# A start through two DMA queues, and 1 MB loads in four pieces

## The chip, the cores and the metric

The kernel runs on one core of a Trainium2 chip. The core has a matmul engine (TensorE; PE in the profile, and PEld for its weight loads), a vector engine (VectorE, DVE), a scalar engine for activations (ScalarE, ACT), GpSimd (POOL) and a sync engine (SP) that does little but issue transfers. ACT can issue transfers too, in line with its other instructions (ACTq in the profile). Each engine takes its instructions strictly in the order written, and waits for others by semaphores. Transfers move through 16 DMA engines between the main memory, in which inputs, outputs and scratch lie, and the on-chip memory (SBUF); matmul results land in eight banks of PSUM, from where DVE or ACT copies them out. The metric is the device time of one execution in microseconds.

## The reference: what is computed

The input x is 2048 tokens by 1024 features in bf16. Four blocks follow one another, each a residual step on the normalised x: A, B, A, B, with the weights of A and B used twice. `_layernorm` has no learned scale.

```python
x = A_x
x = x + _A_ref(_layernorm(x, axis=-1), A_wqkv, A_w_phi, A_wo)
x = x + _B_ref(_layernorm(x, axis=-1), B_wqkv, B_wo)
x = x + _A_ref(_layernorm(x, axis=-1), A_wqkv, A_w_phi, A_wo)
x = x + _B_ref(_layernorm(x, axis=-1), B_wqkv, B_wo)
return x
```

A is linear attention with 32 heads of 32 features: queries and keys go through a small matrix phi per head, then softmax over the features of that and of its negative gives 64 features; the state is the sum over tokens of these features times values, and each query reads the state and divides by its own sum. B is ordinary softmax attention over all 2048 tokens with 32 heads of 32, without a mask. Each block ends in a 1024 x 1024 projection.

## The kernel before

x is held transposed on the chip (`xT`: features on the 128 partitions in 8 groups `po`, tokens along the row), and the tokens are worked in 4 chunks of 512 (`C512`). One pass over A then B is called a layer here; there are two. All other on-chip data lie in one big tile, `arena`, in which a small allocator places buffers; a buffer's class has a quota and a queue.

The start, which the change touches most:

- `load_x` brings x in by transposing transfers. Chunk 0 is 8 transfers of 128 x 512, chunk 1 another 8, and chunks 2 and 3 together 8 of 128 x 1024, all on SP (L516).
- `fold_phi` for the keys loads the key weights in two halves of 1 MB through ACT's queue (L604), transposes them on PE in 8 groups g (L613), casts each group out of PSUM (L621 on ACT, L618 on DVE), multiplies with phi (L640) and casts the results into two slabs of folded weights (L647 on ACT, L650 on DVE). The slabs are also stored to scratch (L654) for layer 2. Queries are folded the same way later, with transposing transfers (L627) in the place of PE's transposes.
- `slab` loads a slab of weights, 128 x 8 x 512 (1 MB) or 128 x 8 x 128 (256 KB), as one transfer on SP (L585). Its third result is a list of four dependencies, one for each pair of the 8 groups `po`; before, all four are the same transfer.
- `layernorm` of a chunk squares x on ACT (L539) in `n` parts, sums x and its squares over the features by matmuls with a constant matrix (L481 with onesD), forms the inverse deviation (L560 to L567) and applies it on DVE in four pairs of steps (L573, L577). With n=4 the first part starts when its quarter of x is there; with n=2 there are two parts.
- `a_keys` of a chunk: for two halves of the features and four groups of 128 tokens, keys and values by matmuls (L481), exponentials on ACT (L689), sums, reciprocals and scaled values on DVE (L693 to L702), and the state by small matmuls (L722).

After A's queries and projection come B's keys, queries and values, and the attention loop: scores (L1105) into PSUM, exponentials on ACT (L1114, some on DVE by a polynomial, L1048 to L1062), and products with the values and sums (L1146). Between these the planner fits matmuls of other work (L485). While layer 1's attention runs, layer 2's A already takes the keys of chunks 0 to 2; their normed chunks are stored to scratch (L1372) and loaded again when needed (L1263, 1 MB each).

The order of all instructions is the work of a planner at build time. Each piece of work is an `op` with an engine, an assumed duration, a priority (a due time) and its dependencies and buffers. `Sched.run` steps through an assumed time, and whenever an engine is free it takes the ready op with the lowest priority whose buffers can be placed. For transfers it assumes a fixed latency of 2 us and one that grows with the size (`kb`), partly in one line for all queues. The instructions are then issued in the order found, so any change to an op's pieces, sizes or priorities can move work anywhere behind it. What the planner assumes of times enters the order only. Semaphore waits follow from the data, and from eight semaphores which transfers use in turn: a transfer waits until the last one with its semaphore has landed.

Of the kernel before, what the change touches and what calls it, by code (L numbers as in the profile page):

```python
# [20 lines left out]
C512 = 512  # L21
# [315 lines left out]
def kernel(  # L337
# [11 lines left out]
    nc = tc.nc  # L349
# [44 lines left out]
    for j in range(4):  # L394
# [4 lines left out]
        out=rep[:].rearrange("p (x j) -> p x j", j=4),  # L399
        in_=J_bf[:].rearrange("p (j d) -> p d j", d=32)[:, 0:8, :],  # L400
    )
    nc.vector.tensor_copy(out=fold[:], in_=ident[:, 0:32])
    for a in range(1, 4):
        nc.vector.tensor_tensor(
            out=fold[:], in0=fold[:], in1=ident[:, 32 * a:32 * a + 32], op=ALU.add
# [4 lines left out]
        out=selb[:].rearrange("p (j d) -> p j d", d=32),  # L410
        in_=pick[:].unsqueeze(2).to_broadcast([P, 4, 32]),
    )
    for a in range(4):
        for j in range(4):
            c = (j + a) % 4
            nc.vector.tensor_copy(
                out=selr[32 * a:32 * a + 32, 32 * c:32 * c + 32], in_=selb[32 * a:32 * a + 32, 32 * j:32 * j + 32])
# [18 lines left out]
    xd_v = xd[:].rearrange("p (c o n) -> p c o n", c=3, o=PO)  # L436
# [31 lines left out]
    ANY = [(x,) for x in (7, 6, 5, 4, 3, 2, 1, 0)]  # L468
# [6 lines left out]
    def dma(prio, fn, deps=(), bufs=(), q="SP", kb=256, issue=0.55):  # L475
        return op(q, issue, fn, deps, bufs, prio, lat=2.0 + kb / 200.0)
# [34 lines left out]
    def load_x():  # L511
        for lo, hi, prio, us, kb in ((0, 1, -24.0, 1.3, 128), (1, 2, -9.0, 1.3, 400), (2, NC, -8.0, 2.0, 800)):
            last = []
            for po in range(PO):
                last.append(dma(
                    prio, lambda lo=lo, hi=hi, po=po: nc.sync.dma_start_transpose(  # L516
                        out=xT[:, po, lo * C512:hi * C512], in_=A_x[0, lo * C512:hi * C512, po * P:(po + 1) * P]),
                    issue=us, kb=kb))
            for c in range(lo, hi):
                xdone[c] = last  # L520

# [60 lines left out]

    def slab(cls, prio, src, n, deps=(), q="SP"):
        b, v = sb(cls, PO, n)
        o = dma(prio, lambda: (nc.sync if q == "SP" else nc.scalar).dma_start(out=v(), in_=src),  # L585
                deps, [b], q=q, kb=2 * n)
        return b, v, [o] * 4


    def slab_turned(cls, prio, src, n):  # L590
# [9 lines left out]
    def fold_phi(col, wd_v, prio, use_pe):  # L600
        w_t = []
        if use_pe:
            nb, nv = sb("wnat", PO, D)
            ld = [dma(-20.0, lambda h=h: nc.scalar.dma_start(  # L604
                out=nv()[:, :, C512 * h:C512 * h + C512], in_=A_w[:, :, col + C512 * h:col + C512 * h + C512]),
                (), [nb], q="AQ", kb=1024) for h in range(2)]
            for g in range(G):
                tb, tv = ps("wt", ANY)

                def tr(g=g, tv=tv):  # L610
                    o = tv().bitcast(BF16)
                    for po in range(PO):
                        nc.tensor.transpose(  # L613
                            out=o[:, po * P:(po + 1) * P], in_=nv()[:, po, g * P:(g + 1) * P], identity=ident[:])
                t1 = op("PE", 8 * 0.11, tr, [ld[g // 4]], [tb, nb], prio, mode="n")
                wb, wv_ = sb("wT", D)
                if g % 2:
                    t2 = op("DVE", dve_us(1024), lambda tv=tv, wv_=wv_: nc.vector.tensor_copy(  # L618
                        out=wv_(), in_=tv().bitcast(BF16)), [t1], [tb, wb], prio)
                else:  # L620
                    t2 = op("ACT", act_us(1024), lambda tv=tv, wv_=wv_: nc.scalar.copy(  # L621
                        out=wv_(), in_=tv().bitcast(BF16)), [t1], [tb, wb], prio)
                w_t.append((wb, wv_, t2))
        else:
            for g in range(G):
                wb, wv_ = sb("wT", D)
                t2 = dma(prio, lambda g=g, wv_=wv_: nc.sync.dma_start_transpose(  # L627
                    out=wv_(), in_=A_wqkv[:, col + g * P:col + (g + 1) * P]), (), [wb], issue=1.6)
                w_t.append((wb, wv_, t2))
        slabs = []  # L630
        for fc in range(2):
            s_b, s_v = sb("slab", PO, C512)
            parts = []
            for m in range(PO):
                pb, pv = ps("wt", ANY)

                def fn(m=m, pv=pv, fc=fc):
                    for k in range(4):
                        g = 4 * fc + k
                        nc.tensor.matmul(  # L640
                            pv()[:, k * P:(k + 1) * P], lhsT=w_t[g][1]()[:, m * P:(m + 1) * P],
                            rhs=phi()[:, g, :], start=True, stop=True)
                a = op("PE", 4 * 0.1, fn, [w_t[4 * fc + k][2] for k in range(4)] + phi_ld,
                       [pb, phi_b] + [w_t[4 * fc + k][0] for k in range(4)], prio + 0.01, mode="n")
                eng = ("ACT", "DVE")[m % 2]
                if eng == "ACT":
                    e = op("ACT", act_us(512), lambda m=m, pv=pv, s_v=s_v: nc.scalar.copy(  # L647
                        out=s_v()[:, m, :], in_=pv()), [a], [pb, s_b], prio + 0.01)
                else:
                    e = op("DVE", dve_us(512), lambda m=m, pv=pv, s_v=s_v: nc.vector.tensor_copy(  # L650
                        out=s_v()[:, m, :], in_=pv()), [a], [pb, s_b], prio + 0.01)
                parts.append(e)
            fs = slice(fc * C512, (fc + 1) * C512)
            st = dma(prio + 0.02, lambda s_v=s_v, fs=fs: nc.sync.dma_start(out=wd_v[:, :, fs], in_=s_v()),  # L654
                     parts, [s_b], kb=1024)
            slabs.append((s_b, s_v, [[parts[2 * i], parts[2 * i + 1]] for i in range(4)], st))
        return slabs
# [554 lines left out]
    xnA, xnB = {}, {}  # L1212
# [20 lines left out]
    for layer in range(2):  # L1233
# [14 lines left out]
            wv_s = [wv_slab(base + fc * 0.5, fc) for fc in range(2)]  # L1248
            chunks = range(NC - 1, NC)
        for c in chunks:  # L1250
            xnA[c] = layernorm(c, base + 10 * c - 9 if base + c else -16.0, ANY, n=4 if layer else 2)
            a_keys(c, base + 10 * c, wk_s, wv_s, kv, ANY)
        state = a_state(kv, base + 32)

        if layer == 0:
            wq_s = fold_phi(0, wdq_v, base + 15, False)
            store["q"] = [s[3] for s in wq_s]
        else:
            wq_s = [slab("slab", second - 15 + fc, wdq_v[:, :, fc * C512:(fc + 1) * C512], C512, [store["q"][fc]])
                    for fc in range(2)]  # L1260
            for c in range(NC - 1):
                x_b, x_v = sb("xn", PO, C512)
                xnA[c] = (x_b, x_v, [dma(second - 20 + 20 * c, lambda c=c, x_v=x_v: nc.sync.dma_start(  # L1263
                    out=x_v(), in_=xd_v[:, c, :, :]), [xnA[c]], [x_b], kb=1024)] * 4)
        wo_s = [slab_turned("slab", second - 6 + fc, A_o[:, :, fc * C512:(fc + 1) * C512], C512) for fc in range(2)]
        bv_s = [slab("slab", second - 4 + 134 * fc, B_w[:, :, 2 * D + fc * C512:2 * D + (fc + 1) * C512], C512)
                for fc in range(2)]
# [149 lines left out]
```

## Time and profile before

| what | value |
|---|---|
| median of 3 runs | 2376.43 us (2372.92 to 2377.3) |
| profiled execution | 2378.41 us, span 2376.6 us |
| granted matmul clock, mean | 0.994 |
| busy share of the span | PE 94%, ACT 87%, DVE 69%, POOL 1% |
| transfers | 118.58 MB, mean 50 GB/s |

A row of the instructions in time has the start in us, the duration, the engine, the line, what is written from what, how many follow each other (x), and in brackets how long the engine sat idle before and what ended that. A row of the waits has the waiter, what it waited for, the total in us, how often, and the longest. A row of busy time by stretch has, for each engine, busy us and the number of instructions, then the granted clock, the share of time in which the DMA engines were busy, and GB/s. "issue" is time in which an engine waited for nothing that the profile shows.

### The profile page before, as it was taken

What the parts mean: (1) busy time and instruction counts of PE and PEld (TensorE: products, weight loads), DVE (VectorE), ACT (ScalarE), POOL (GpSimd) and SP (SyncE); (2) the same over time, 40 slices, a digit from 0 to 9 for tenths busy, and PEclk for the clock granted to TensorE, in tenths of its full rate; (3) what the DMA queues carried; (4) which work ended last, traced back from release to release, by engine and by line L of the source; (5) the groups of instructions that cost most, each with busy time, mean ns of one, the idle gap of its engine ahead of it and who ended that gap; (6) DMA issues with size and microseconds to landing.
All of it is one profiled execution on the core that took longest, in us unless ns stands there. A gap on an engine that the chain in (4) does not pass through costs nothing. (4 is left out here: it accounts for less than half of the span.)

```text
span 2376.6 us, 65432 instructions
## 1 busy us (share of the span) xinstructions
PE 2243.0 (94%) x28906; PEld 846.6 (36%) x28976; DVE 1647.7 (69%) x2111; ACT 2073.2 (87%) x1852; POOL 25.4 (1%) x70
## 2 busy tenths in 40 slices
PE   7999999999999998999998999999999999989998
PEld 4443343333333333333333444433333333333333
DVE  7987752345678676775754786477778888978763
ACT  5436559999999999999996555899999999999998
POOL 0000000000000000000000000000000000000000
PEclk9999999999999999999999999999999999999999
DMA  9210101112221222213313101011111100111111
GB/s 217 64 34 1 32 21 33 28 38 64 63 80 54 56 60 69 82 56 91 126 56 98 37 3 34 22 36 27 35 26 38 34 20 24 56 35 36 38 36 38
DMA packets 218085, 118.58 MB, mean 50 GB/s; under 512 B 139208, under 2 KB 208840, under 8 KB 217032
## 3 DMA queue, kind: packets, MB, share of 16 engines
q1 hardware_dynamic: 215720, 112.29, 17.6%
q8 instruction: 226, 3.70, 0.6%
q10 hardware_dynamic: 2080, 2.10, 0.3%
q14 instruction: 59, 0.48, 0.1%
HBM read 78.71 MB, written 14.14 MB: 39 GB/s over the span
## 5 line engine op out<-in xcount | busy, mean ns | idle before, releaser
L1114 ACT ACTIVATE arena<-psum 128x1536 bf16<-128x1536 f32 x1297 | 1752.8, 1699 | 18.5 <-PE psum L1105 15.9
L1146 PE MATMUL psum<-arena 128*32 128x512 bf16 x4096 | 629.2, 385 | 11.8 <-DVE arena L1162 10.3
L1146 PE MATMUL psum<-arena,ones_bf 128*32 128x512 bf16 x4096 | 628.9, 385 | 0.0
L1105 PE MATMUL psum<-arena 32*128 32x512 bf16 x3890 | 512.8, 383 | 80.2 <-ACT arena L1114 70.3
L485 PE MATMUL psum<-arena 128*32 128x512 bf16 (+1 forms) x8768 | 580.7, 376 | 8.3 <-DVE arena L991 2.5
L481 PE MATMUL psum<-arena 128*128 128x512 bf16 (+1 forms) x1969 | 445.2, 374 | 10.1 <-issue 3.7
L1105 PEld LDWEIGHTS <-arena 32*128 32x128 bf16 x3890 | 173.4, 91 | 584.3 <-issue 573.9
L1059 DVE SCALAR_TENSOR_TENSOR arena<-arena 128x1024 f32<-128x1024 f32 x309 | 376.8, 1220 | 4.2 <-DMA arena<-arena 0.2
L485 PEld LDWEIGHTS <-arena 128*32 128x32 bf16 x8768 | 195.4, 96 | 236.0 <-issue 117.1
L481 PEld LDWEIGHTS <-arena 128*128 128x128 bf16 x2032 | 190.3, 98 | 243.3 <-issue 44.7
L1146 PEld LDWEIGHTS <-arena 128*32 128x32 bf16 x4096 | 167.0, 95 | 253.8 <-issue 198.5
L1048 DVE TENSOR_SCALAR arena<-psum 128x512 int32<-128x512 f32 x206 | 141.8, 688 | 102.0 <-PE psum L1041 91.2
L921 DVE CAST arena<-psum 128x512 bf16<-128x512 f32 x120 | 82.6, 688 | 176.5 <-PE psum L485 167.4
L1146 PEld LDWEIGHTS <-ones_bf 128*32 128x32 bf16 x4096 | 163.5, 95 | 31.8 <-issue 13.1
L1062 DVE SCALAR_TENSOR_TENSOR arena<-arena 128x1024 bf16<-128x1024 f32 x103 | 125.9, 1222 | 3.4 <-PE psum L1146 0.2
L689 ACT ACTIVATE arena<-psum 128x512 bf16<-128x512 f32 x80 | 43.0, 597 | 87.5 <-PE psum L481 66.6
L1381 PE MATMUL psum<-xT,zero 128*32 128x512 bf16 x1428 | 116.9, 383 | 0.0
L1162 DVE COPY arena<-psum 128x512 f32<-128x512 f32 x126 | 86.3, 685 | 34.3 <-PE psum L1146 33.7
L1203 DVE TENSOR_TENSOR arena<-arena 64x512 bf16<-64x512 f32 x124 | 84.7, 683 | 29.7 <-DMA arena<-rd 24.0
L693 DVE TENSOR_REDUCE arena<-arena 128x32 f32<-128x1024 bf16 x64 | 77.6, 1213 | 28.6 <-ACT arena L689 28.4
L815 ACT ACTIVATE arena<-psum 128x512 bf16<-128x512 f32 x128 | 69.4, 598 | 31.3 <-PE psum L481 29.1
L573 DVE TENSOR_TENSOR arena<-xT,arena 128x1024 f32<-128x1024 bf16 x64 | 77.8, 1219 | 23.8 <-ACT arena L562 23.8
(102 smaller groups left out, 1369.2 us busy)
## 6 DMA issues: line engine op xcount, KB each, us to landing
arena<-rd SPq DMA_DIRECT2D x62, 256.0 KB
arena<-in_B_wqkv_dram SPq DMA_DIRECT2D x48, 256.0 KB
arena<-in_A_wqkv_dram SPq DMA_DIRECT2D x10, 1024.0 KB
arena<-arena SPq DMA_DIRECT2D x256, 32.0 KB
arena<-in_B_wo_dram SPq DMA_DIRECT2D x32, 256.0 KB
arena<-wd_k SPq DMA_DIRECT2D x8, 1024.0 KB
arena<-arena SPq DMA_DIRECT2D x96, 64.0 KB
arena<-in_B_wqkv_dram SPq DMA_DIRECT2D x4, 1024.0 KB
```

Of the source, the lines that this page charges most:

```text
L481: nc.tensor.matmul(out_, lhsT=lhsT, rhs=rhs, start=start, stop=stop, skip_group_check=True)
L485: nc.tensor.matmul(out_[ks, :], lhsT=lhsT[:, ks], rhs=rhs, start=start, stop=stop, tile_position=(0, 32 * k), skip_group_check=True)
L921: return op("DVE", dve_us(512), lambda: nc.vector.tensor_copy(out=dst(), in_=src()), [dep], bufs, prio)
L1048: ys.append(op("DVE", dve_us(512), lambda k=k, s_v=s_v: nc.vector.tensor_scalar(out=y_v()[:, k, :].bitcast(I32), in0=s_v(), scalar1=POW2_B ...
L1059: last = [op("DVE", dve_us(1024), lambda i=i, c=c: nc.vector.scalar_tensor_tensor(out=x_v(), in0=(x_v() if i else m_v()), scalar=c, in1=m_ ...
L1062: eo = op("DVE", dve_us(1024), lambda: nc.vector.scalar_tensor_tensor(out=e_v(), in0=x_v(), scalar=POW2_0, in1=y_v(), op0=ALU.add, op1=ALU ...
L1105: nc.tensor.matmul(out=s_v()[:, x * C512:(x + 1) * C512], lhsT=kT[g][1]()[r, pp, d * P:(d + 1) * P], rhs=q_of[(qc, g)][1]()[r, (pp + j // ...
L1114: ex = op("ACT", act_us(w * C512), lambda s_v=s_v, e_v=e_v, w=w: nc.scalar.activation(out=e_v()[:, 0:w * C512], in_=s_v(), func=ACT.Exp, s ...
L1146: nc.tensor.matmul(out=a_v()[col:col + 32, :], lhsT=v_v()[:, kc % 4, o:o + DH] if what == 0 else ones_bf[:], rhs=ev()[:, x * C512:(x + 1) ...
L1162: cp = op("DVE", dve_us(512), lambda t_v=t_v, a_v=a_v: nc.vector.tensor_copy(out=t_v(), in_=a_v()), [last], [a_b, t_b], prio - 4)
L1203: s = [op("DVE", dve_us(512), lambda a=a, k=k, o_v=o_v, r_v=r_v, T=T: nc.vector.tensor_tensor(out=o_v()[a, :], in0=T[k][1]()[a, :], in1=r_ ...
L1381: nc.tensor.matmul(psum[32 * k:32 * k + 32, 6 * C512:7 * C512], lhsT=zero[:], rhs=xT[:, 0, 0:C512], start=False, stop=False, tile_position ...
```

## The change

Four edits:

- In `load_x`, the odd ones of the eight transposing transfers of chunk 0 are issued from ACT's queue ("AQ"), the even ones from SP's.
- In the first `layernorm`, chunk 0 of layer 1 is squared in four parts (n=4), each part with the transfers of its own quarter as dependency, and the sums wait quarter by quarter.
- In `slab`, a load of 1 MB becomes four transfers of 256 KB, each for a pair of groups, and each matmul waits only for its own; so do the reloads of the stored chunks in layer 2 (L1263). The priorities of the four differ by 0.001.
- In `fold_phi`, of the eight casts of transposed key weights only the last is on DVE, seven are on ACT; before, four and four.

```diff
             for po in range(PO):
+                q = "AQ" if lo == 0 and po % 2 else "SP"
                 last.append(dma(
-                    prio, lambda lo=lo, hi=hi, po=po: nc.sync.dma_start_transpose(
+                    prio, lambda lo=lo, hi=hi, po=po, q=q: (nc.sync if q == "SP" else nc.scalar).dma_start_transpose(
                         out=xT[:, po, lo * C512:hi * C512], in_=A_x[0, lo * C512:hi * C512, po * P:(po + 1) * P]),
-                    issue=us, kb=kb))
+                    q=q, issue=us, kb=kb))
...
     def slab(cls, prio, src, n, deps=(), q="SP"):
         b, v = sb(cls, PO, n)
-        o = dma(prio, lambda: (nc.sync if q == "SP" else nc.scalar).dma_start(out=v(), in_=src),
-                deps, [b], q=q, kb=2 * n)
-        return b, v, [o] * 4
+        if n < C512:
+            o = dma(prio, lambda: (nc.sync if q == "SP" else nc.scalar).dma_start(out=v(), in_=src),
+                    deps, [b], q=q, kb=2 * n)
+            return b, v, [o] * 4
+        return b, v, [dma(prio + 0.001 * i, lambda i=i: (nc.sync if q == "SP" else nc.scalar).dma_start(
+            out=v()[:, 2 * i:2 * i + 2, :], in_=src[:, 2 * i:2 * i + 2, :]),
+            deps, [b], q=q, kb=n / 2) for i in range(4)]
...
-                if g % 2:
+                if g == 7:
                     t2 = op("DVE", dve_us(1024), lambda tv=tv, wv_=wv_: nc.vector.tensor_copy(
...
-            xnA[c] = layernorm(c, base + 10 * c - 9 if base + c else -16.0, ANY, n=4 if layer else 2)
+            xnA[c] = layernorm(c, base + 10 * c - 9 if base + c else -16.0, ANY, n=4 if layer or c == 0 else 2)
...
-                xnA[c] = (x_b, x_v, [dma(second - 20 + 20 * c, lambda c=c, x_v=x_v: nc.sync.dma_start(
-                    out=x_v(), in_=xd_v[:, c, :, :]), [xnA[c]], [x_b], kb=1024)] * 4)
+                xnA[c] = (x_b, x_v, [dma(second - 20 + 20 * c + 0.001 * i, lambda c=c, x_v=x_v, i=i: nc.sync.dma_start(
+                    out=x_v()[:, 2 * i:2 * i + 2, :], in_=xd_v[:, c, 2 * i:2 * i + 2, :]),
+                    [xnA[c]], [x_b], kb=256) for i in range(4)])
```

## The prediction

> **What bounds the kernel now.** I read the page first, then the busy time by stretch, the list of waits of the matmul engine, and the instructions of the first 62 us in order of time.
>
> ```profile
> span 2376.6 us, 65432 instructions
> PE 2243.0 (94%) x28906; PEld 846.6 (36%) x28976; DVE 1647.7 (69%) x2111; ACT 2073.2 (87%) x1852; POOL 25.4 (1%) x70
> ...
> core 0: us, PE busy (x) PEld busy (x) DVE busy (x) ACT busy (x) POOL busy (x), PEclk, DMA share, GB/s
> 0.00:40.00 40.00, 27.61 (x194) 17.66 (x198) 25.72 (x60) 22.90 (x29) 1.02 (x7) 0.96 0.99 228
> 40.00:360.00 320.00, 313.78 (x2788) 137.54 (x2824) 245.75 (x313) 161.97 (x268) 10.03 (x31) 1.00 0.17 40
> 360.00:1220.00 860.00, 814.67 (x11910) 287.11 (x11906) 531.83 (x672) 854.59 (x671) 11.47 (x23) 1.00 0.22 62
> 1220.00:1300.00 80.00, 69.91 (x861) 24.57 (x856) 37.89 (x49) 62.41 (x53) 0.34 (x1) 0.89 0.37 110
> ```
>
> From 40 to 360 us (the first linear-attention block) PE is busy 313.78 of 320 us; from 360 to 1220 (softmax attention) ACT is busy 854.59 of 860. Neither stretch has room: a delay that enters at 40 us comes out at the end almost whole. The first 40 us are another matter: PE has 12.4 us of idle there, and the DMA engines are full (0.99).
>
> ```profile
> PE psum L1105 <- ACT arena L1114: 70.3, 221, 1.0
> PE psum L1146 <- DVE arena L1162: 10.3, 28, 0.9
> PE psum L613 <- DMA arena<-in_A_wqkv_dram: 9.4, 2, 6.6
> ```
>
> Among the waits of PE, just two are for a transfer, 9.4 us in all: the two halves of the key weights at the very start (L613). No other weight load is ever waited for by PE.
>
> ```profile
> 0.74 10.40 SPq L516 DMA_TRANSPOSE xT<-in_A_x_dram  x8
> 0.76 6.76 ACTq L604 DMA_DIRECT2D arena<-in_A_wqkv_dram  x2
> 6.59 3.59 PE L613 MATMUL psum<-ident,arena 128*128 128x128 bf16 x32 [6.59 <-DMA arena<-in_A_wqkv_dram]
> 7.66 1.01 ACT L621 COPY arena<-psum 128x1024 bf16<-128x1024 bf16 x1 [5.65 <-PE psum L613]
> 8.52 0.69 DVE L618 COPY arena<-psum 128x1024 bf16<-128x1024 bf16 x1 [2.84 <-PE psum L613]
> 11.25 1.99 SPq L1216 DMA_DIRECT2D arena<-in_A_w_phi_dram  x4
> 12.95 3.28 PE L613 MATMUL psum<-ident,arena 128*128 128x128 bf16 x32 [2.77 <-DMA arena<-in_A_wqkv_dram]
> 13.28 1.08 SPq L585 DMA_DIRECT2D arena<-in_A_wqkv_dram  x2
> 14.41 18.67 SPq L516 DMA_TRANSPOSE xT<-in_A_x_dram  x12
> 16.07 1.89 PE L481 MATMUL psum<-xT,onesD 128*128 128x512 bf16 x7
> 21.20 2.07 ACT L647 CAST arena<-psum 128x512 bf16<-128x512 f32 x4
> 23.21 0.72 ACT L565 ACTIVATE arena<-arena,eps 128x512 f32<-128x512 f32 x1
> 23.96 0.63 ACT L567 ACTIVATE arena<-arena 128x512 f32<-128x512 f32 x1
> 24.82 2.35 DVE L577 TENSOR_TENSOR arena<-arena 128x1024 bf16<-128x1024 f32 x2
> 30.74 1.23 DVE L577 TENSOR_TENSOR arena<-arena 128x1024 bf16<-128x1024 f32 x1
> 31.88 2.48 DVE L650 CAST arena<-psum 128x512 bf16<-128x512 f32 x4
> 35.11 13.54 PE L481 MATMUL psum<-arena 128*128 128x512 bf16 x60
> 36.26 1.22 DVE L693 TENSOR_REDUCE arena<-arena 128x32 f32<-128x1024 bf16 x1 [0.26 <-ACT arena L689]
> ```
>
> So before: the key weights are issued at 0.76 us, land by 6.59 and 12.95, are transposed (L613) and cast (L621, L618) by 17 us, folded with phi into two slabs (L640, casts L647 and L650), and by 35.11 us PE runs the keys of chunk 0 without a gap.
>
> **The change part by part.**
>
> *The transposed loads of chunk 0.* The eight go out alternately on SP and ACT. In the order of the changed kernel's instructions the two queues don't run side by side: ACT's first transpose waits for the landing of SP's first three, SP's fourth waits for ACT's first, and ACT's second waits for SP's fourth. So it is a chain with three hand-overs, each of an issue and a landing. One issue takes 10.40/8 = 1.30 us. The landing behind an issue is not seen for transposes; from below, a small transfer in a quiet stretch:
>
> ```profile
> 386.47 1.18 SPq L1192 DMA_DIRECT2D arena<-arena  x2
> 388.85 0.25 DVE L1197 RECIPROCAL arena<-arena 128x16 f32<-128x16 f32 x1 [2.41 <-DMA arena<-arena]
> ```
>
> 388.85 - 387.65 = 1.2 us. From above: the last issue ended at 11.14 and PE read xT at 16.07, at most 4.9 us, with weights in the same rings. At the start of the changed kernel the rings are nearly empty, so I take 1.5. Then SP's three are issued by 4.6 and landed at 6.1; ACT's first 7.4, landed 8.9; SP's fourth 10.2, landed 11.7; ACT's last three are issued by 15.6 and landed at 17.1. The chunk lands no earlier than before (use at 16.07).
>
> The Trainium skill, "DMA: Bandwidth & Descriptors", section "Silent corruption: two transposing streams in flight at once", says that a stream's first transpose must wait until the other stream's have fully landed. The chain of waits above is that rule carried out; no run here shows what happens without it.
>
> *What is queued behind them on ACT.* The weight loads of L604 stand behind ACT's four transposes, the first also behind the first Square. They are issued at about 15.6 instead of 0.76. With the landing times of the rows (6.59 - 0.76 = 5.8 us for the first, the second some 4 us behind it because it shares the engines) they land at 21.4 and 25.5: +14.8 and +12.6 us.
>
> *Casts.* Seven of the eight go to ACT now (four before), 1.01 us each, with the norm's Ln and Exp (0.72 + 0.63) among them: from 21.4 + 1.07 = 22.5 to 22.5 + 7.1 + 1.4 = 31.0. DVE loses three (2.07 us) but its one remaining cast stands behind the eight norm steps, which start after Exp at 24.9 and take what they took before (24.82 to 31.97, 7.15 us): 32.0, the cast 32.7, then eight L650 at 0.69. PE's last fold matmul waits for the sixth of them: 36.9 us. ACT's eight L647 (0.59) run beside this.
>
> *Norm by quarters.* Four Squares instead of two; a quarter takes 1.06 us in layer 2's first norm:
>
> ```profile
> 1285.46 1.06 ACT L539 ACTIVATE arena<-xT 128x1024 bf16<-128x1024 bf16 x1 [2.98 <-DVE xT L994]
> ```
>
> That is 4.2 us instead of 3.71 (the row at 53.62 below). They lie before the weights land, where ACT has nothing else: 0, and 0.5 us if the weights came early.
>
> *Keys of chunk 0.* At 36.9 PE has 66 + 46 matmuls of 128x512 left up to the norm of chunk 1; at 35.06 before it had 62 + 36. (The early value matmuls, which wait for a quarter of the value weights only, fill 16 of PE's gaps.) At 13.54/62 = 0.217 us: 36.9 - 35.1 + 14 x 0.217 = 4.8 us late.
>
> *Chunk 1 and the SP queue.* SP's third and fourth quarters of the value weights wait for the two late key loads (they reuse their semaphores), to 25.5, and four more issues follow (1.08/2 = 0.54 each); chunk 1's transposes start at about 28, not 14.41. At 18.67/12 = 1.56 us the fourth is landed at 28 + 6.2 + 1.5 = 35.7. ACT's Square of it stands ahead of the last two L647 and is reached at 31.0 + 6 x 0.59 = 34.5: 1.2 us more, held against the casts PE waits for. Sum of the start: **+6.0 us**; between 4.9 (landing 1.2 us, no wait here) and 16 (landing 4.9 us: the weights would be issued at 25.8).
>
> ```profile
> 37.21 7.15 SPq L516 DMA_TRANSPOSE xT<-in_A_x_dram  x3
> 44.46 11.77 SPq L627 DMA_TRANSPOSE arena<-in_A_wqkv_dram  x8
> 53.62 3.71 ACT L539 ACTIVATE arena<-xT 128x2048 bf16<-128x2048 bf16 x2
> 61.08 0.39 PE L640 MATMUL psum<-arena 128*128 128x128 bf16 x4
> ```
>
> Chunks 2 and 3 were issued by 44.4 and used at 53.62; now by 57.5, landed at 59, used at 53.62 + 6 = 59.6: hidden by half a microsecond, and every further one shows. The query weights' first four transposes now land at 57.5 + 4 x 1.47 + 1.5 = 64.9, their first use is 61.08 + 6 = 67: hidden.
>
> *Loads in four pieces.* 83 more issues on SP at about 0.5 us. PE waits for none of these loads, so the earlier first quarter gains nothing: 0. The issues are hidden by SP's own idle time; without that cover a small transfer queued behind a load, and DVE waiting for it, comes 3 x 0.54 = 1.6 us later. What can move is traffic: while two 1 MB loads land, PE stands still for no visible reason and ACT after it:
>
> ```profile
> 1225.18 1.00 SPq L585 DMA_DIRECT2D arena<-wd_q  x2
> 1235.50 1.04 PE L485 MATMUL psum<-xT,onesD 128*32 128x512 bf16 x5 [2.96 <-issue]
> 1237.61 1.45 ACT L1114 ACTIVATE arena<-psum 128x1536 bf16<-128x1536 f32 x1 [3.15 <-PE psum L1105]
> ```
>
> The pieces go out nearly back to back, the same bytes; I take 0, with 3.2 us either way.
>
> *The planner's new order.* The same work stands in another order in places up to the end. From 60 us on ACT has the same instructions, a few in other places, and it is what bounds the attention; I take 0, and 3 us either way.
>
> **Sum.** The profiled execution took 2378.4 us; +6.0 from the start, and I add 0.6 for chunk 2's cover of half a microsecond, which I don't expect to hold every time: 2385.0. The profiled execution lies 2.0 above the median of the runs, 2376.4; against the median the same +6.6 gives **2383.0**.
>
> **The rivals.**
> 1. *The queues run at once after all* (not slower). ACT's four issues would be over at 0.74 + 5.2 = 5.9, the weights issued 9.7 us earlier than I say, and everything behind them: -9.7 + 6.6 = -3.1, 2373. It decides from the point where the hand-overs cost under a third of my 1.5 us plus issue. For it: nothing but the wish; against it: the waits. The Trainium skill, same page, section "Issuing engines are not separate DMA queues", holds that a second issuing engine only saves issue time; that saving is the 5.2 us used here, and the rows agree that issue (1.30 us each) paces these loads.
> 2. *The delay is eaten* (no change). DVE is freed of 2.07 us of casts, the norm is done ahead of the keys, or the stall at 1232 goes away (3.15): 2383.0 - 3.2 = 2380, within 0.2%. 0.2% of 2376 is 4.8 us, about what a measurement of this kernel can tell from no change. Against it: PE's 313.78 of 320.
> 3. *The delay grows.* The landing is nearer 3 us than 1.5 (three hand-overs, +4.5), or chunk 2 comes later than its Square and holds ACT's exponentials: 2388 to 2393.
>
> **How the numbers follow.** My forecast, a start 5 to 9 us later that stays: 0.53 (2381 to 2386). Growing: 0.17. Eaten: 0.20. Queues at once, or a new order that gains more than the start loses: 0.10. Slower by over 0.2% (above 2381.2): 0.69; within: 0.22; faster: 0.09. The range goes from 2375 (rival 2 with 3 us of order on top) to 2392 (most of rival 3).
>
> **What would show it.** In the changed kernel's trace: ACT's first L604 issue near 15.6 us and the first L613 matmul at 21 to 22, waiting for the transfer; the chunk's transposes on SP in a group of three and one with a gap of 4 us; PE gapless in L481 from 37 to 39; DVE's first key sum (L693, 36.26 before) near 42; ACT busy as before from 370. Wrong if L613 starts before 12 us, if PE's busy share between 20 and 40 us rises, or if the second attention block differs by more than the start does.

## The result, and the profile after

The changed kernel takes 2379.98 us (median of 13 runs), the kernel before 2375.81 us (13 runs beside it). The ratio is 1.0024 with a 95% interval of 1.0017 to 1.0031: 4.0 to 7.4 us slower, 5.7 in the middle (the medians differ by 4.2). The forecast was 2383.0, or +6.6. The profiled execution took 2382.2 us (span 2380.4), 2.2 above its median; the one of before (2378.4) lies 2.6 above the median of its 13 runs. Single executions of either kernel differ by some 8 us, so what follows about places in one trace is firm where it is a start time in the first 360 us, and soft where it is a difference of 2 or 3 us late in the run. The changed kernel's lines lie one to six further down from L516 on: L516 is L517, L604 is L609, L613 is L618, L621 is L626, L650 is L655, L693 is L698, L722 is L727, L1105 is L1110, L1114 is L1119, L1146 is L1151.

The page of the changed kernel, and its busy time by the same stretches as those of before:

```profile
span 2380.4 us, 65541 instructions
PE 2238.2 (94%) x28917; PEld 842.3 (35%) x28984; DVE 1646.0 (69%) x2108; ACT 2075.1 (87%) x1857; POOL 23.1 (1%) x70
```

```profile
0.00:40.00 40.00, 23.78 (x178) 13.14 (x181) 20.08 (x54) 21.11 (x27) 0.70 (x6) 1.00 0.67 160
40.00:360.00 320.00, 313.16 (x2765) 137.14 (x2800) 249.34 (x316) 161.00 (x269) 10.39 (x32) 1.00 0.21 48
```

In the first 40 us PE does 23.78 us of work where it did 27.61, and the busy share of the DMA engines is 0.67 instead of 0.99, in the one stretch that lives on transfers. From 40 to 360 us PE is as full as before (313.16 against 313.78), so there is nowhere to win it back.

The instructions of the changed kernel in order of time, at the start:

```profile
0.74 9.03 SPq L517 DMA_TRANSPOSE xT<-in_A_x_dram  x4
6.04 8.83 ACTq L517 DMA_TRANSPOSE xT<-in_A_x_dram  x4
14.94 1.20 ACTq L609 DMA_DIRECT2D arena<-in_A_wqkv_dram  x2
16.56 0.58 PE L481 MATMUL psum<-xT,onesD 128*128 128x512 bf16 x1 [0.58 <-DMA xT<-in_A_x_dram]
21.16 1.51 PE L618 MATMUL psum<-ident,arena 128*128 128x128 bf16 x24 [0.82 <-DMA arena<-in_A_wqkv_dram]
24.02 5.57 ACT L626 COPY arena<-psum 128x1024 bf16<-128x1024 bf16 x6
24.91 1.67 PE L618 MATMUL psum<-ident,arena 128*128 128x128 bf16 x24 [1.43 <-DMA arena<-in_A_wqkv_dram]
27.34 14.05 SPq L517 DMA_TRANSPOSE xT<-in_A_x_dram  x10
31.81 4.86 DVE L655 CAST arena<-psum 128x512 bf16<-128x512 f32 x8
33.40 2.52 PE L645 MATMUL psum<-arena 128*128 128x128 bf16 x32
35.97 5.99 PE L481 MATMUL psum<-arena 128*128 128x512 bf16 x27
39.63 1.22 DVE L698 TENSOR_REDUCE arena<-arena 128x32 f32<-128x1024 bf16 x1 [2.95 <-ACT arena L694]
43.20 8.36 PE L481 MATMUL psum<-arena 128*128 128x512 bf16 x37 [1.25 <-ACT arena L694]
59.78 1.91 ACT L540 ACTIVATE arena<-xT 128x2048 bf16<-128x2048 bf16 x1 [0.65 <-DMA xT<-in_A_x_dram]
66.53 1.36 PE L727 MATMUL psum<-arena 128*32 128x33 bf16 x128
```

The two queues take turns. SP's first three go out, ACT's first at 6.04, SP's fourth after that, ACT's other three until 14.87, and only then, at 14.94, the key weights, which went out at 0.76 before. They are used from 21.16 and 24.91 (before: 6.59 and 12.95). Everything that hangs on them is late: the last folds at 33.4 to 35.9, the keys of chunk 0 behind them. The mark that I use below is the second block of 128 small state matmuls (L722 before, L727 here), which closes the keys of chunk 0. Here it starts at 66.53, before at 61.40: **5.1 us late**.

From there the delay travels. The same instruction in both traces: the first exponential of the attention at 357.3 instead of 352.2 (+5.1), the one 500 further on at 1052.8 instead of 1043.6 (+9.2), the end of layer 1's attention at 1284.9 instead of 1281.2 (+3.7), and the last division of layer 2's at 2369.0 instead of 2365.6 (+3.4). The regain sits at the end of layer 1, where the standstill of before is gone. ACT of the changed kernel in that place:

```profile
1232.91 6.92 ACT L1119 ACTIVATE arena<-psum 128x1536 bf16<-128x1536 f32 x5
1239.57 1.30 ACT L694 ACTIVATE arena<-arena 128x512 bf16<-128x512 f32 x2
1240.61 12.32 ACT L1119 ACTIVATE arena<-psum 128x1536 bf16<-128x1536 f32 x9
```

Before, ACT stood still for 3.15 us ahead of 1237.61, after PE had stood still for 2.96; the granted clock was 0.79 from 1232 to 1236 us and 0.50 from 1236 to 1240. Here ACT runs through, and the clock is 1.00 in the same places.

### The profile page after: what moved, and what is told of

It reads as the page before. It is cut to its first block, busy times and chain, and to the rows that moved or that the text cites. A ratio compares the mean times of both kernels' runs of the same rounds, so it can differ in the third digit from the quotient of the medians.

```text
span 2380.4 us, 65541 instructions
## 1 busy us (share of the span) xinstructions
PE 2238.2 (94%) x28917; PEld 842.3 (35%) x28984; DVE 1646.0 (69%) x2108; ACT 2075.1 (87%) x1857; POOL 23.1 (1%) x70
## 5 line engine op out<-in xcount | busy, mean ns | idle before, releaser
L1119 ACT ACTIVATE arena<-psum 128x1536 bf16<-128x1536 f32 x1297 | 1751.6, 1685 | 15.8 <-PE psum L1110 9.8
L1151 PE MATMUL psum<-arena 128*32 128x512 bf16 x4096 | 624.8, 384 | 10.6 <-DVE arena L1167 8.9
L1151 PE MATMUL psum<-arena,ones_bf 128*32 128x512 bf16 x4096 | 625.1, 385 | 0.0
L485 PE MATMUL psum<-arena 128*32 128x512 bf16 (+1 forms) x8768 | 579.4, 375 | 13.3 <-DVE arena L926 3.3
L1110 PE MATMUL psum<-arena 32*128 32x512 bf16 x3890 | 512.3, 383 | 83.8 <-ACT arena L1119 73.3
L1110 PEld LDWEIGHTS <-arena 32*128 32x128 bf16 x3890 | 173.9, 91 | 588.3 <-issue 577.3
L485 PEld LDWEIGHTS <-arena 128*32 128x32 bf16 x8768 | 194.7, 96 | 240.7 <-issue 121.7
L1151 PEld LDWEIGHTS <-arena 128*32 128x32 bf16 x4096 | 166.2, 95 | 248.9 <-issue 193.4
L1151 PEld LDWEIGHTS <-ones_bf 128*32 128x32 bf16 x4096 | 162.8, 95 | 30.7 <-issue 12.0
L698 DVE TENSOR_REDUCE arena<-arena 128x32 f32<-128x1024 bf16 x64 | 77.7, 1215 | 39.8 <-ACT arena L694 36.7
```

The source lines that it names most:

```text
L485: nc.tensor.matmul(out_[ks, :], lhsT=lhsT[:, ks], rhs=rhs, start=start, stop=stop, tile_position=(0, 32 * k), skip_group_check=True)
L1110: nc.tensor.matmul(out=s_v()[:, x * C512:(x + 1) * C512], lhsT=kT[g][1]()[r, pp, d * P:(d + 1) * P], rhs=q_of[(qc, g)][1]()[r, (pp + j // ...
L1119: ex = op("ACT", act_us(w * C512), lambda s_v=s_v, e_v=e_v, w=w: nc.scalar.activation(out=e_v()[:, 0:w * C512], in_=s_v(), func=ACT.Exp, s ...
L1151: nc.tensor.matmul(out=a_v()[col:col + 32, :], lhsT=v_v()[:, kc % 4, o:o + DH] if what == 0 else ones_bf[:], rhs=ev()[:, x * C512:(x + 1) ...
```

## The experiments

Two theories. **Start**: the two queues wait for each other's landing, the key weights stand behind that on ACT, and the time follows the start. **Order**: the planner writes another order for everything behind the change, and that order, not the start, makes the time. Each ratio is against the kernel before, run beside it.

**1. One queue again, the rest of the change kept** (`x_on_sp`).

```diff
-                q = "AQ" if lo == 0 and po % 2 else "SP"
+                q = "SP"
```

> The changed kernel with all eight transposes of chunk 0 on SP again; norm by quarters, casts and pieces stay. Theory (the late key weights make the delay): the first L613 transposes begin at 6.6 us again, the second block of state matmuls (L722: 61.4 us before, 66.5 after the change) begins at 60 to 62 us, the first exponential of the attention (352.2 and 357.3) at 351 to 353, and the whole is 4 to 6 us faster than the changed kernel, 2373 to 2377 us. Rival (the pieces on SP or the seven casts on ACT make it): the second state block stays at 65 us or later and the whole within 2 us of the changed kernel.

Measured: ratio 1.0000 (0.9991 to 1.0009). The start of this kernel in order of time:

```profile
0.76 6.79 ACTq L609 DMA_DIRECT2D arena<-in_A_wqkv_dram  x2
6.63 3.60 PE L618 MATMUL psum<-ident,arena 128*128 128x128 bf16 x32 [6.63 <-DMA arena<-in_A_wqkv_dram]
61.32 1.20 PE L727 MATMUL psum<-arena 128*32 128x33 bf16 x128
```

The weights go out at 0.76 again, the second state block is back at 61.32, and the whole loss is gone. But the planner wrote a new order here too, so this alone can't tell the two theories apart.

**2. The second queue alone** (`two_queues_only`): the kernel before with only the edit of `load_x`. Its lines lie one further down than before.

> The kernel before with the two queues for chunk 0 alone. Theory: key weights issued near 15 us, second state block at 65 to 68 us, the whole 4 to 7 us slower than before. Rival (pieces or casts): no more than 2 us slower than before.

Measured: ratio 1.0077 (1.0063 to 1.0091), 18 us, three times the whole change and far outside both of my expectations. Its start:

```profile
24.81 1.89 PE L614 MATMUL psum<-ident,arena 128*128 128x128 bf16 x16 [4.42 <-DMA arena<-in_A_wqkv_dram]
37.84 1.28 DVE L619 COPY arena<-psum 128x1024 bf16<-128x1024 bf16 x2
75.01 1.20 PE L723 MATMUL psum<-arena 128*32 128x33 bf16 x128
```

The key weights go out as late as in the changed kernel (15.21), but PE first uses them at 24.81, 3.65 us later than there (21.16). Beside them SP has sent the value weights in two whole loads of 1 MB (at 15.26 and 16.78); in the changed kernel only two pieces of 256 KB were out before 21.13. I put the 3.65 us down to the DMA engines that these loads share; no run changes that alone. Then their casts are still half on DVE and ordered around the norm steps there: the last three start at 37.84 or later, where the changed kernel has its folding done. The second state block comes at 75.01, 13.6 us late. So the other parts of the change, pieces, quarters and casts, with the order that they lead to, take back 8.5 us of the start that the second queue loses.

**3. The key weights ahead of ACT's transposes** (`weights_first`): in the changed kernel, their priority is raised so that they go out first.

```diff
-            ld = [dma(-20.0, lambda h=h: nc.scalar.dma_start(
+            ld = [dma(-30.0, lambda h=h: nc.scalar.dma_start(
```

> The changed kernel with the key weights' due time moved ahead of the transposes, so that both L604 loads are issued on ACT before ACT's transposes; the two queues stay, with one hand-over (four on SP, then four on ACT). Theory (what costs is the place of the weights behind the transposes, not the two queues as such): first L613 at 6 to 7 us, the last quarter of chunk 0 at about 16 to 18 us, second state block at 60 to 63 us, the whole 3 to 6 us faster than the changed kernel. Rival (the two queues cost by their waits wherever the weights stand): second state block at 65 us or later, the whole within 2 us of the changed kernel.

Measured: ratio 1.0070 (1.0058 to 1.0083). I had expected it to beat the changed kernel; it is 11 us slower. The start, and the passage from the last keys of the softmax block to its first scores:

```profile
0.74 5.62 SPq L517 DMA_TRANSPOSE xT<-in_A_x_dram  x4
6.67 2.74 PE L618 MATMUL psum<-ident,arena 128*128 128x128 bf16 x24 [6.67 <-DMA arena<-in_A_wqkv_dram]
11.44 5.18 ACTq L517 DMA_TRANSPOSE xT<-in_A_x_dram  x4
16.66 1.93 ACT L626 COPY arena<-psum 128x1024 bf16<-128x1024 bf16 x2 [14.64 <-issue]
69.40 1.20 PE L727 MATMUL psum<-arena 128*32 128x33 bf16 x128 [0.69 <-DVE arena L707]
...
345.73 18.29 PE L481 MATMUL psum<-arena 128*128 128x512 bf16 x82
365.79 0.60 PE L1110 MATMUL psum<-arena 32*128 32x512 bf16 x6
```

Two things went wrong. The second state block is 8.0 us late. The weights are there at 6.67 and the first group is transposed by 7.6, but ACT casts nothing until 16.66: its own four transposes stand ahead of the casts and wait for SP's to land, and while it waits to issue them it computes nothing. Of the 14.64 us that ACT was idle ahead of 16.66, some 9 are that wait and those issues. The one hand-over left costs 5.1 us (from the end of SP's issues at 6.36 to 11.44), since SP's transposes land behind 2 MB of weights in flight; in the changed kernel a hand-over takes 1.3 to 1.5. And later the planner put all 82 matmuls of the last keys ahead of the first scores; before, it was 51 (340.21 to 351.5), and the first exponential came between the others. That costs 8.5 us more (the first exponential is 14.0 late, the residual sums in front of it 5.5). The first is the start theory with a new place; the second is the order theory.

**4. The 1 MB loads whole again** (`whole_loads`): the changed kernel without its edits of `slab` and of the reloads. Its lines lie one further down than before.

> The changed kernel with loads of 1 MB in one piece again; two queues, quarters and casts stay. Theory: the start stays late (second state block 65 to 68 us, first exponential 356 to 359). If the pieces also made up for time in the attention of layer 1 (the changed kernel's delay shrinks from 5.1 us at the first exponential to 3.7 at the end of that attention), the delay at its end is 5 us or more and the whole 1 to 3 us slower than the changed kernel; if that gain is chance of the order, it is within 1.5 us either way.

Measured: ratio 1.0143 (1.0129 to 1.0157), 34 us, by far the largest effect of all. The second state block is 9.7 us late (the change: 5.1). Nearly all of the difference is there when PE first uses the key weights, at 25.30 against 21.16: they went out 0.5 us later (15.44) and, as in `two_queues_only`, had whole loads of value weights beside them. The largest part of the rest enters in one place. The first use of the key weights, then PE and ACT between 717 and 728 us:

```profile
25.30 3.54 PE L614 MATMUL psum<-ident,arena 128*128 128x128 bf16 x32 [4.07 <-DMA arena<-in_A_wqkv_dram]
...
722.11 0.83 PE L1382 MATMUL psum<-xT,zero 128*32 128x512 bf16 x12
723.09 1.91 PE L485 MATMUL psum<-arena 128*32 128x512 bf16 x32
727.97 2.79 ACT L1115 ACTIVATE arena<-psum 128x1536 bf16<-128x1536 f32 x2 [11.01 <-DMA arena<-arena]
```

ACT has no scores to work on for 11.01 us. PE is computing the keys and queries that they need (L485) and they then travel by small transfers. Between them stand L1382 matmuls, which multiply by zero: the planner puts them where it knows of nothing else to do. So this gap was planned, not met by chance on the chip. The kernel before has whole loads too, and no such gap: it comes with this order, not with whole loads as such.

**5. The changed kernel's own order, on one queue** (`same_order_on_sp`). Here the planner still takes the four transposes for ACT's queue, so the order on every engine is the changed kernel's, but they are issued on SP.

```diff
-                    prio, lambda lo=lo, hi=hi, po=po, q=q: (nc.sync if q == "SP" else nc.scalar).dma_start_transpose(
+                    prio, lambda lo=lo, hi=hi, po=po, q=q: nc.sync.dma_start_transpose(
```

> The changed kernel with its whole order on every engine kept (the planner still takes the four transposes for ACT's queue), but those four are issued on SP, so no stream waits for the other's landing. Theory A (the hand-overs are the delay, and the rest of the new order costs nothing): the key weights go out before 2 us and land by 7 and 13, the second block of state matmuls comes back from 66.5 to about 61.4 us, and the time is 2374 to 2377, that is 3 to 6 below the changed kernel and at or below the kernel before. Rival B (the order that the planner wrote for a late chunk is what costs): the start is early but engines wait in that order all the same, second state block at 65 or later, and the time stays at 2379 to 2382.

Measured: ratio 1.0003 (0.9994 to 1.0012), span of the profiled execution 2375.6. Its start:

```profile
0.73 10.43 SPq L517 DMA_TRANSPOSE xT<-in_A_x_dram  x8
4.66 0.45 ACTq L609 DMA_DIRECT2D arena<-in_A_wqkv_dram  x1
16.48 1.55 PE L618 MATMUL psum<-ident,arena 128*128 128x128 bf16 x24
60.15 1.34 PE L727 MATMUL psum<-arena 128*32 128x33 bf16 x128
```

This is the run that settles it. With the order held, taking the second queue away brings the second state block from 66.53 to 60.15 and the ratio from 1.0024 to 1.0003. The loss is the second queue, and the changed kernel's order costs nothing that shows by itself (the start is 1.25 us earlier than before, 60.15 against 61.40, and the time is not shorter). In this trace too ACT runs through the place at 1237 us, so the standstill of before went with the order, not with the queues. The same holds for the growth and the regain in the changed kernel's trace: in the four places named above (the first exponential, the one 500 further on, the ends of the two layers' attention) this run lies at -1.3, +2.3, -2.2 and -1.4 against before, so that the changed kernel lies 6.4, 6.9, 5.9 and 4.8 behind it.

**6. No hand-over, but the weights still behind the transposes** (`act_all`), **7. two hand-overs, one transpose on ACT** (`act_one`). Order as in the changed kernel; `k` counts the transposes as they go out. The lines lie eight further down.

```diff
+        sent = []
+
+        def queue(lo, rule):
+            if lo:
+                return nc.sync
+            sent.append(0)
+            return nc.scalar if rule(len(sent) - 1) else nc.sync
...
-                    prio, lambda lo=lo, hi=hi, po=po, q=q: (nc.sync if q == "SP" else nc.scalar).dma_start_transpose(
+                    prio, lambda lo=lo, hi=hi, po=po, q=q: queue(lo, lambda k: True).dma_start_transpose(
```

For `act_one` the rule is `k == 3`.

> The changed kernel with its order kept, but all eight transposes of the first chunk on ACT's queue: no hand-over between two streams is left, while the key weights still stand behind the transposes on ACT. Theory A (the hand-overs are part of the delay, the place in ACT's queue the rest): eight issues of 1.25 to 1.3 us end at about 11, the weights go out at 11 to 12.5 instead of 14.9 and 15.6, the second state block lies near 63 us (66.5 changed, 60.1 with all eight on SP in this order), and the profiled time lies 3 to 4 us below the changed kernel, 2376 to 2378. Rival F (the hand-overs are hidden and only the place behind the transposes costs): the same 66 us and 2379 to 2382 as the changed kernel. Rival G (only the hand-overs cost): 60 to 61 us and 2374 to 2376.

> The changed kernel with its order kept and only one of the eight transposes on ACT's queue (the fourth to go out): two hand-overs of SP's stream to ACT and back, but only one transpose ahead of the key weights on ACT. Theory A: ACT's transpose is issued at 6.0 and SP goes on at 8.6; the first half of the weights is out at about 8.5, the second near 10 to 12 behind the second Square; the second state block at 61 to 63 us; 2375 to 2378 by the profile. Rival G (each hand-over costs the end about 2 us wherever it stands): two thirds of the changed kernel's delay, 64 to 65 us and 2379.

Measured: 1.0016 (1.0007 to 1.0026) for all eight on ACT, 1.0028 (1.0019 to 1.0038) for one on ACT. The starts, first of the kernel with all on ACT, then of the one with one on ACT:

```profile
0.76 10.46 ACTq L525 DMA_TRANSPOSE xT<-in_A_x_dram  x8
11.35 1.14 ACTq L617 DMA_DIRECT2D arena<-in_A_wqkv_dram  x2
62.97 1.30 PE L735 MATMUL psum<-arena 128*32 128x33 bf16 x128
```

```profile
0.74 14.92 SPq L525 DMA_TRANSPOSE xT<-in_A_x_dram  x7
7.47 0.56 ACTq L617 DMA_DIRECT2D arena<-in_A_wqkv_dram  x1
18.55 1.52 PE L481 MATMUL psum<-xT,onesD 128*128 128x512 bf16 x3 [9.11 <-DMA xT<-in_A_x_dram]
20.23 0.58 PE L481 MATMUL psum<-xT,onesD 128*128 128x512 bf16 x1 [0.16 <-DMA xT<-in_A_x_dram]
68.11 1.20 PE L735 MATMUL psum<-arena 128*32 128x33 bf16 x128
```

Without hand-overs the eight issues take 10.46 us on ACT as they take 10.43 on SP, the weights follow at 11.35, and the second state block comes at 62.97, as theory A of the expectation said. Of the 6.4 us between 60.15 and 66.53, 2.8 are so the place behind the transposes, and 3.6 the hand-overs; the next run shows that the two don't simply add. The time agrees less well: the profiled execution lies 0.9 below the changed kernel's, not 3 to 4, and the ratio falls by 0.0008, within the intervals.

The kernel with one transpose on ACT refutes what I expected. Its weights go out from 7.47 on, long before the changed kernel's, and its start is the worst of this order, 68.11. The last four transposes on SP now share the DMA engines with 2 MB of weights: the last two take 2.0 and 2.2 us to issue instead of 1.3, the first of the four, issued by 9.95, lands only at 18.5, and PE uses the last of the chunk at 20.23, against 16.56 in the changed kernel. In this order the sums over x stand ahead of the weights' transposes on PE, and it waits 9.11 us for the first of the four. So early weights are worth nothing to an order that wants x first, and cost what they take from x.

**8. Half of the casts on DVE, same order** (`same_order_casts_half`). Its lines lie one further down than the changed kernel's.

```diff
-                    t2 = op("ACT", act_us(1024), lambda tv=tv, wv_=wv_: nc.scalar.copy(
+                    t2 = op("ACT", act_us(1024), lambda g=g, tv=tv, wv_=wv_: (
+                        nc.vector.tensor_copy if g % 2 else nc.scalar.copy)(
```

> The changed kernel with its order kept, but the second, fourth and sixth of the eight casts of the key weights' transposes run on DVE instead of ACT, at the same place between its neighbours. Theory A (once the weights are late, DVE with its norm steps is what the folding waits for, so the casts on ACT save what they took from DVE): the last fold casts on DVE end 1 to 2 us later, second state block near 68 us, time 1 to 2 us above the changed kernel. Rival H (the share of the casts doesn't matter): within 0.5 us of 66.5 and the same time. Rival I (ACT's column of casts is what the folding waits for): 1 to 3 us earlier, 64 to 65 us.

Measured: ratio 1.0025 (1.0015 to 1.0035), the same as the change. Its rows:

```profile
33.42 4.87 DVE L656 CAST arena<-psum 128x512 bf16<-128x512 f32 x8
66.97 1.31 PE L728 MATMUL psum<-arena 128*32 128x33 bf16 x128
```

DVE's fold casts start 1.6 us later (33.42 against 31.81), as theory A said, but only 0.4 us of it reaches the second state block. The share of the casts hardly matters as long as the order stays; for what `two_queues_only` lost beside the queue this points to the later landing of its key weights and to the place of DVE's casts in the order, rather than to their engine. The five kernels of this one order:

| transposes on ACT | hand-overs | first weights out | second state block | ratio |
|---|---|---|---|---|
| 0 | 0 | 4.66 | 60.15 | 1.0003 |
| 8 | 0 | 11.35 | 62.97 | 1.0016 |
| 4 (the change) | 3 | 14.94 | 66.53 | 1.0024 |
| 4, casts half on DVE | 3 | 15.19 | 66.97 | 1.0025 |
| 1 | 2 | 7.47 | 68.11 | 1.0028 |

The time rises with the start, over 8.0 us of it by 0.0025 (5.9 us).

**9. Pieces in the order of before** (`pieces_same_order`): each 1 MB load is one step for the planner and four transfers of 256 KB on the chip. The reloads alike.

```diff
-        o = dma(prio, lambda: (nc.sync if q == "SP" else nc.scalar).dma_start(out=v(), in_=src),
-                deps, [b], q=q, kb=2 * n)
+        def go():
+            for i in range(4 if n == C512 else 1):
+                k = slice(2 * i, 2 * i + 2) if n == C512 else slice(0, PO)
+                (nc.sync if q == "SP" else nc.scalar).dma_start(out=v()[:, k, :], in_=src[:, k, :])
+        o = dma(prio, go, deps, [b], q=q, kb=2 * n)
```

> The kernel before in its own order, with each 1 MB load issued as four loads of 256 KB one right behind the other; nothing else moves. Prediction's term (pieces are worth nothing by themselves): 2376 to 2379, ratio within 0.001 of 1, and the standstill of PE and ACT at 1232 us as before. Rival C (the pieces change the traffic so that this standstill goes): 2373 to 2375, with ACT busy without a gap from 1230 to 1242. Rival D (83 more issues hold small transfers back on SP): 2380 or more, with more time of ACT or DVE waiting for transfers between 360 and 1220 us.

Measured: ratio 1.0008 (0.9999 to 1.0017): nothing, or up to 4 us lost. At 1237 us ACT still stands still, for 1.73 us instead of 3.15 (the lines lie three further down than before):

```profile
1237.78 1.45 ACT L1117 ACTIVATE arena<-psum 128x1536 bf16<-128x1536 f32 x1 [1.73 <-PE psum L1108]
```

In the order of before the pieces are worth nothing that shows as traffic; there the value weights go out at 13.28, when the last key weights have landed (12.95). That does not carry over to a start with late key weights, where whole value loads stand beside them and the first use comes 3.65 us and more later (experiments 2 and 4). What `whole_loads` lost beyond its start I put down to the order, in which the 11 us gap was planned; the rest of it is not shown.

**10. Norm by quarters and casts alone** (`norm_casts_only`): the kernel before with these two edits.

```diff
-                if g % 2:
+                if g == 7:
...
-            xnA[c] = layernorm(c, base + 10 * c - 9 if base + c else -16.0, ANY, n=4 if layer else 2)
+            xnA[c] = layernorm(c, base + 10 * c - 9 if base + c else -16.0, ANY, n=4 if layer or c == 0 else 2)
```

> The kernel before with the norm of the first chunk by quarters and seven of the eight casts on ACT; one queue, whole loads. Theory A (only the second queue costs): 2375 to 2380, as with one queue and pieces (ratio 1.000). Rival E (the pieces are what lets the planner keep its order; whole loads cost 31 us in the changed kernel): 2385 to 2405, with a gap in ACT's exponentials between 600 and 800 us.

Measured: ratio 1.0039 (1.0027 to 1.0052), with the second state block at 62.34 (0.9 late). The time lies in the range of rival E, but without its gap: the loss arises later than the start, and no single gap in the exponentials carries it.

**11 and 12. Another order of the same work** (`plan_issue_06`, `plan_issue_05`): the kernel before with one number that the planner assumes.

```diff
-    def dma(prio, fn, deps=(), bufs=(), q="SP", kb=256, issue=0.55):
+    def dma(prio, fn, deps=(), bufs=(), q="SP", kb=256, issue=0.6):
```

> The kernel before with one number of the planner's changed: it takes an ordinary transfer's issue for 0.60 us instead of 0.55. The same loads, matmuls, casts and exponentials, in another order. The prediction's term (a new order is worth 3 us at most either way): 2373 to 2380. Rival O (the order alone moves the time by more than the change under study did): off by 5 to 20 us, on either side, with the first exponential or a gap between exponentials moved while the second state block stays at 61.4 us.

> The kernel before with the planner's estimate of an ordinary transfer's issue at 0.50 us instead of 0.55: a second sample of what a new order of the same work is worth (0.60 gave 1.0025 with a start 1.2 us earlier). The prediction's term: within 3 us of before, 2374 to 2380. Rival O (orders scatter by 5 us and more): off by 4 to 15 us on either side, the difference arising after the first exponential.

Measured: 1.0025 (1.0014 to 1.0036) with 0.60, 1.0043 (1.0030 to 1.0056) with 0.50. Not one load or matmul of the work is changed, the second state block lies at 60.23 and 61.99 against 61.40, and the time is 6 and 10 us longer. ACT's waits between 352 and 1285 us, of the kernel before and of the one with 0.50:

```profile
ACT arena L1114 <- PE psum L1105: 9.6, 8, 3.2
ACT arena L1114 <- PE psum L1146: 0.3, 1, 0.3
```

```profile
ACT arena L1114 <- PE psum L1105: 7.8, 9, 2.2
ACT arena L1114 <- PE psum L1146: 7.8, 7, 2.2
```

ACT's exponentials now wait behind products with the values (L1146), 7.5 us more over seven waits, with 1.8 less of waiting for scores (L1105); two waits of its casts and norm add 3.8 more. By the end of layer 1's attention this kernel is 7.5 us late.

No kernel of these is faster than the one before; with one queue the change comes out level with it.

## Why the prediction was right, and where its terms were off

**The hand-overs.** From the rows: the eight issues and three hand-overs end at 6.04 + 8.83 = 14.87; less 0.74 and eight issues of 1.30, three hand-overs take 3.7, or 1.24 us each. I took 1.5, near the lower end of 1.2 to 4.9. About half of the difference is the landing, which the single transfers show 1.31 to 1.36 us behind the end of an issue; the other half is the issues next to a hand-over, some of them shorter (1.12 to 1.14). So the weights went out at 14.94, not 15.6. That the hand-overs wait at all, on which rival 1 hung, is confirmed by the runs with one queue: eight issues take 10.46 us on ACT and 10.43 on SP, and 14.13 when they alternate. The Trainium skill, "DMA: Bandwidth & Descriptors", section "Issuing engines are not separate DMA queues", says that a second issuing engine saves issue time only. Here not even that was saved; what it would save without the waits no run shows, since none has both transposing streams in flight at once.

**The weights.** Used at 21.16 and 24.91; I had 21.4 and 25.5.

**Casts and folds.** ACT's casts ended at 29.6 (I said 31.0), DVE's fold casts began at 31.81 (32.7), and the folds on PE ended at 35.9 (36.9): right in kind, a microsecond early. DVE's first key sum came at 39.63, not near 42. There I had the keys without a gap; PE has one, 1.25 us ahead of 43.20, where the exponentials of the keys stand behind ACT's Square of chunk 1. It is the term of 1.2 us that I had put on the fold's casts, one step further on.

**Chunks 1 and 2.** SP went on with chunk 1 at 27.34 (28). Chunk 2's first Square came at 55.57 and did not wait, where I had 59.6; its second waited 0.65 us for its transfer at 59.78, which is the size of the 0.6 that I had added, at the other half.

**The start's sum.** 5.1 us at the second state block, against 6.0 and 0.6: the step that was mis-sized is the hand-over, 1.24 instead of 1.5, three times, and the folds that follow a little faster. A second difference is hidden in the net: against its own order on one queue the change loses 6.4 us there, and the rest of the change wins 1.25, which the sum did not have as a term of its own. That the net lies within a microsecond or so of the forecast is in part luck. The lower end that I gave the start, 4.9, leaves out that shorter landings also bring the weights 0.9 us forward; by the sum's own terms it is 3.9.

**Loads in pieces.** I took 0, with 3.2 either way. In an unchanged order they are worth 1.0008, which is 0 as far as it can be told. I had not asked what the pieces do to the plan, in which they are dependencies as well as transfers: without them the planner wrote the order with the 11 us gap of `whole_loads`. Nor had I asked what they do to the late key weights: in the two kernels with whole loads those are first used 3.65 and 4.14 us later than in the changed kernel. In the changed kernel this stays hidden, since the change has the pieces.

**The planner's new order.** 0 was right for this order: on one queue it gives 1.0003. The bound of 3 us was wrong. It was argued from ACT's having the same instructions in other places, and the runs show what other places can cost: 6, 9 and 10 us in three orders whose start is within 1.2 us of before, and 24 in `whole_loads` beyond its late start. The forecast came out because this order happened to be a good one, not because orders are worth little. A range with the 10 us of `plan_issue_05` in the place of my 3 would have reached to about 2393 on the slow side from the order alone, and the 24 us of `whole_loads` lie beyond that.

**The rivals.** Rival 1 (queues at once) fell by the waits. Rival 2 (the delay is eaten) had one part right, the standstill at 1237 is gone, and the delay in the single trace shrinks from 5.1 to 3.4 us; the interval of the ratio still leaves 4.0 us at least, and the one-queue run of this order lacks the standstill too without being faster than before. Rival 3 (the delay grows) fell with hand-overs of 1.24 us.

## What to carry to other kernels

A second queue for transposing transfers was no second lane here: each change of queue cost an issue's landing, 1.24 us in the changed kernel and 5.1 where 2 MB of loads were in flight ahead of it, and whatever stood behind on the waiting engine, transfers and compute alike, was late by the whole chain. Where a planner writes the order, compare a change in the old order and in the new one before giving it the credit or the blame; one assumed number of the planner's, which changed no work, moved this kernel by as much as the change did.

## What the runs showed that I had not expected

An engine that issues transfers stops computing while its transfer waits: some 9 us of ACT in `weights_first`, with casts to do. Transposes beside 2 MB of plain loads took up to 2.2 us to issue instead of 1.3 and one of them 8.6 us to land behind its issue instead of 1.3 to 1.4, and weights sent out 7 us earlier made the start 1.6 us later (`act_one`). And the busy share of the DMA engines in the first 40 us, 0.99 before, was 0.86 in the changed kernel's order on one queue and 0.67 with the loads spread over two.
